# Attention and a feed forward on one Trainium2 core: the last four weight combinations in other places, three sum terms in quads 3 to 5, and raw weights behind q and k in quads 3 and 4

## The chip, the core and the metric

The kernel runs on one core of a Trainium2 chip. TensorE (PE in the profile) multiplies matrices and writes to PSUM. VectorE (DVE), ScalarE (ACT) and GpSimd (POOL) work element by element, and SyncE (SP) issues nearly all transfers between HBM and SBUF. Each engine runs its own instructions in order, and waits for others by semaphores. The metric is device time in microseconds (us); lower is better.

## What is computed

```python
# 8 batches, 12 heads, 448 positions, 64 per head; then 3584 tokens, 768 -> 1024 -> 768
q_n, k_n = rmsnorm(q, g_q), rmsnorm(k, g_k)            # over the 64 of a head
scores = matmul(q_n, k_n^T) / sqrt(64)
attn = softmax(scores);  x = matmul(attn, v)           # heads side by side: 3584 x 768
h = x @ w_in
solu = h * softmax(h)
ln = (solu - mean(solu)) / sqrt(var(solu) + 1e-6) * g_ln
out = ln @ w_out
```

The attention's inputs are float32; w_in and w_out come as float64 and are turned into float32 on the chip.

## The kernel before

**Two stages.** Attention works on 24 *quads* of four heads (m = 0 to 23, three quads per batch). The feed forward then works through 3584 tokens. Both feed forward products are done by a Strassen-like scheme: seven products of half-size blocks in place of eight. For that w_in is kept as seven blocks: three quarters of w_in itself, and four differences of quarters. The differences are made by twelve *combinations* on GpSimd (`combine_in(x)`, x = 0 to 11, L572), subtractions of 128 x 512 elements that have to be done before the first feed forward product.

**A quad** (the loop at L1561). TensorE computes the scores of seven groups of keys (`both_scores`, L870; a group is called 0 to 6), ScalarE takes the exponentials E (L839) straight from PSUM, and TensorE multiplies them by v and accumulates over the seven groups in one PSUM accumulator `o` (`both_values`, L884). There is one buffer for `o`, so the first value product of quad m + 1, which comes behind four scores, has to wait until VectorE has copied `o` of quad m to SBUF as `xo` (`take`, L986). SP then writes it to memory (`store_x`, L993).

**The sums of a row of exponentials** are not divided out here. VectorE adds E tiles of a quad into a few *terms* (`add_pair` L896, `add_to` L902), and TensorE multiplies the terms of one to three quads by ones in one *phase* (`sums`, L941; `end_sums`, L1553) behind the values of the last of them. ScalarE copies the result (`keep_sums`, L957) and SP stores it. In quads 1 to 5 a quad has four terms (E0+E1+E2, E3+E4, E5, E6), from quad 6 on three (E0+E1+E2+E3, E4+E5, E6). Phases stand behind quad 0, quad 2 (quads 1 and 2), quad 4 (3 and 4), quad 5 (5 alone), and then behind every third quad, 8 to 23 (`sums_at`). When a batch is complete its sums are loaded again (`load_sums`), inverted on VectorE (`invert`, L979) and sent to memory (`send_inverses`). x is multiplied by them in the feed forward (`scale`, L1043; x and the inverses of the first tokens are loaded in quads 22 and 23, L1713 to L1720).

**q and k** arrive in eight pieces a quad of 112 KB (`load_piece`, L638). They are squared on ScalarE (`squares`, L687), summed on VectorE (`row_sums`, L692), folded on GpSimd (`fold_sums`, L700), turned into an inverse root on ScalarE and VectorE (`rsqrt_seed` L705, and the norm step `rsqrt_step` L716, four short VectorE instructions), multiplied on GpSimd (`normalise`, L725) and transposed on VectorE (`qk_transpose`, L747). Up to quad 5 the squares and row sums that stand in quad m, between its first scores, are those of quad m + 2. From quad 6 on (`early`) the row sums stand ahead of the scores; the squares for quad m + 3 stand at the end of quad m, from quad 5 on. In quads 3, 4 and 5 ten pieces are loaded each (`load_pieces(10)`, L1646).

**The weights** of w_in come in twelve raw tiles of 512 KB, loaded by `load_next` (L1469) in the quad m for which m + 2 is in `steps_at` (5, 6, 8, 9, ... 21) and converted two quads later by two ScalarE and two VectorE instructions (`convert_w`; the last, `join`, L545 and L546, writes w_in).

**The order is written out by hand.** All of this stands in one program order, and each engine and the SP queue take their part of it in that order. Ahead of a quad's first scores stand, in this order: the load of v for the next quad, the combination if the quad has one (*beside*, L1582 to L1591), `take` of the quad before, its stores, inverses, the raw load (L1603), then the norm step, `normalise` for the next quad, and the q and k pieces. The combinations 0 to 7 stand in quads 11, 12, 14, 15, 17, 18, 20 and 21, one each, *beside* the take: GpSimd first copies one element that VectorE's last work of the quad before has written (`pass_on`, L569), so that the combination begins behind that work, and the program puts `take(m - 1)` ahead of the norm step on VectorE. In the other quads from 6 on the norm step comes ahead of `take`. Quad 22 has four: 8 and 9 without a gate, ahead of the `normalise` of quad 23 (L1639), and 10 and 11 behind the scores' first half (L1678). There the order on VectorE is norm step, then take(21). Quad 23 has none.

Of the kernel before, what the change touches and what calls it, by code (L numbers as in the profile page):

```python
# [366 lines left out]
def fast_path(  # L367
# [32 lines left out]
    NQ = B * NP // 2  # L400
# [171 lines left out]
    def combine_in(x):  # L572
        c, i = divmod(x, 4)
        combine([w_in[k][:, c] for k in range(7)], i)
# [150 lines left out]
    def normalise(n, e=nc.gpsimd):  # L725
        d = st[n]
        y = norms[n // 2]["y"][:, n % 2 * 2 * NB : (n % 2 + 1) * 2 * NB]
        d["qkn"] = work.tile([P, 2 * NB, 32], FP32, tag="qkn", name="qkn", bufs=2)
        e.tensor_tensor(  # L729
            d["qkn"].rearrange("p (s b) d -> p s b d", s=2),  # L730
            d["qk"].rearrange("p s (b d) -> p s b d", d=32),
            y.rearrange("p (s b) -> p s b ()", s=2).to_broadcast([P, 2, NB, 32]),
            OP.mult,
        )
# [718 lines left out]
    EARLY = 6  # L1453
    steps_at = (5, 6, 8, 9, 11, 12, 14, 15, 17, 18, 20, 21)
    combines_at = {11 + 3 * (x // 2) + x % 2: (x,) for x in range(8)}
    combines_first = {22: (8, 9)}
    combines_at[22] = (10, 11)
    sums_at = (2, 4, 5) + tuple(range(8, NQ, 3))
    inverts_at = {4: (0,), 8: (1,), 10: (2,), 14: (3,), 16: (4,), 20: (5,), 22: (6,)}
    wq += [(moe_w_out, c + k, i) for c in range(HF) for k in (0, HF) for i in range(2)]  # L1460
    again = [(w, w.shape[0] // P, i) for w in (moe_w_in, moe_w_out) for i in range(-(-w.shape[0] // P * w.shape[1] // S))]
# [7 lines left out]
    def load_next():  # L1469
        if len(raws) < (n_in if conv is None else len(wq)):  # L1470
            raws.append(load_w(wq[len(raws)]))
# [13 lines left out]
    def load_pieces(n):  # L1485
        nonlocal pieces
        n = min(n, 8 * NQ - pieces)
        for _ in range(n):
            load_piece(pieces)
            pieces += 1  # L1490

    with tc.manual_schedule():
# [68 lines left out]
        for m in range(1, NQ):  # L1561
            a, b = 2 * m, 2 * m + 1
            next1 = m + 1 < NQ
            next2 = m + 2 < NQ
            early = EARLY <= m
            four = m < EARLY

            def score(x):
                unit(lambda: both_scores(m, x))

            def value(x):
                unit(lambda: both_values(m, x))

            if m == 3:
                norm_gain()
            sent = None
            if kept:
                sent = keep_sums(*kept)
                kept = None
            if next1:  # L1580
                load_v(m + 1)
            beside = combines_at.get(m, ()) if m < 22 else ()  # L1582
            if beside:
                if m - 1 in steps_at:
                    step = wq[steps_at.index(m - 1)]
                    pass_on(w_in[(0, 3, 1, 2)[step[1] // HD * 2 + step[2]]][0:1, step[1] % HD, 0:1])
                else:
                    pass_on(quads[m - 1]["terms"][2][1][0:1, 0, 0:1])
                for x in beside:
                    combine_in(x)  # L1590
                take(m - 1)  # L1591
            if early and next1:
                rsqrt_step(norms[m + 1])
            if m > 1 and not beside:
                take(m - 1)
            store_x(m - 1)
            if sent:
                sent()
            for x in inverts_at.get(m - 1, ()):
                send_inverses(x)  # L1600
            for x in inverts_at.get(m, ()):
                load_sums(x)
            if m + 2 in steps_at:  # L1603
                load_next()
            if m == 1:
                score(0)
                score(1)
                score(2)
                rsqrt_seed(norms[2])
                rsqrt_step(norms[2])  # L1610
                normalise(4)
                normalise(5)
                load_pieces(8)
                score(3)
                squares(6)
                row_sums(6)
                qk_transpose(4)
                value(0)
                score(4)
                squares(7)  # L1620
                row_sums(7)
                qk_transpose(5)
                value(1)
                score(5)
                fold_sums(3)
                value(2)
                score(6)
                gains(2)
                rsqrt_seed(norms[3])
                add_pair(m, 0, 1)  # L1630
                add_to(m, 0, 2, nc.vector)
            else:
                if next1:
                    if not early:
                        rsqrt_step(norms[m + 1])
                    if m == 2:
                        add_pair(1, 3, 4)
                        quads[1]["terms"].append((2, quads[1]["E", 5]))
                    for x in combines_first.get(m, ()):  # L1639
                        combine_in(x)  # L1640
                    normalise(a + 2)
                    normalise(b + 2)
                if early:
                    load_pieces(2)
                else:
                    load_pieces(10)  # L1646
                if early and next2:
                    row_sums(a + 4)
                    row_sums(b + 4)
                    load_pieces(6)  # L1650
                if m == NQ - 1:
                    scale(0)
                score(0)
                if m > 2 and not early:
                    squares(a + 4)
                    row_sums(a + 4)
                score(1)
                if next1:
                    qk_transpose(a + 2)
                if m > 2 and not early:  # L1660
                    squares(b + 4)
                    row_sums(b + 4)
                if m == 2:
                    score(2)
                    squares(a + 4)
                    row_sums(a + 4)
                    score(3)
                    squares(b + 4)
                    row_sums(b + 4)
                    qk_transpose(b + 2)  # L1670
                else:
                    if next1:
                        qk_transpose(b + 2)
                    score(2)
                    score(3)
                if next2:
                    fold_sums(m + 2)
                if not beside:  # L1678
                    for x in combines_at.get(m, ()):
                        combine_in(x)  # L1680
                value(0)
                score(4)
                if m in steps_at:
                    low_bits, join, product = convert_w(wq[steps_at.index(m)], raws[steps_at.index(m)])
                    low_bits[0]()
                value(1)
                score(5)
                if m in steps_at:
                    low_bits[1]()
                if next1 and early and m not in sums_at:  # L1690
                    gains(m + 1)
                add_pair(m, 0, 1)
                add_to(m, 0, 2, nc.vector)
                if not four:
                    add_to(m, 0, 3, nc.vector)
                    add_pair(m, 4, 5)
                else:
                    add_pair(m, 3, 4)
                value(2)
                score(6)  # L1700
                if next1 and (not early or m in sums_at):
                    gains(m + 1)
                if m in steps_at:
                    join()
                if next2:
                    rsqrt_seed(norms[m + 2])
                if m + 1 >= EARLY and m + 3 < NQ:
                    squares(a + 6)
                    squares(b + 6)
                if four:  # L1710
                    quads[m]["terms"].append((2, quads[m]["E", 5]))
            quads[m]["terms"].insert(0, (2, quads[m]["E", NK - 1]))
            if m == NQ - 2:  # L1713
                load_x(0)
                load_r(0)
            if m == NQ - 1:
                load_x(1)
                sizes(0)
                block_sums(0, 0)
                block_sums(0, 1)  # L1720
            for x in inverts_at.get(m, ()):
                invert(x)
            for x in range(3, NK):
                value(x)
            waiting.append(m)
            if m in sums_at:
                unit(lambda: None)
                kept = end_sums()
                waiting.clear()
# [62 lines left out]
        for n in range(NS):  # L1792
            base = period * n
            for i, name in enumerate(ORDER):
# [4 lines left out]
                x = HALVES[name][0]  # L1799
# [118 lines left out]
```

## Time and profile before

| | us |
|---|---|
| median of 3 timed runs (lowest, highest) | 786.2 (786.06, 786.36) |
| the profiled execution | 786.86 |
| its span, first to last instruction | 784.2 |
| TensorE busy | 773.3 |
| VectorE busy | 605.9 |
| ScalarE busy | 508.8 |
| GpSimd busy | 485.3 |

The granted TensorE clock is 0.998 over the span, so a TensorE instruction of one shape takes the same time everywhere.

How to read the rows. A row of a timeline has the start in us from the span's start, the duration, the engine, the line of the kernel, the operation, out<-in by the program's names, shapes, and xN where N records are merged. A float32 product leaves two records, so x32 for the scores is 16 products, four groups of keys. A bracket at the end is the idle time of the engine before it and what ended it. A row of groups has the busy time in us, the mean of one in ns, and behind the second bar the idle time before the group with its releasers. In the chain of waits "x64" counts products and weight loads. Names: s are scores, o the accumulator of the values, xo its copy, es the terms of the sums, sm the sums in PSUM, sq squares, ss and part their sums, nx and ny the norm step, qkn and qkT the normalised and the transposed q and k, inv the inverses, raw the float64 weights.

### The profile page before, as it was taken

Reading aid. Unit: us, or ns where it says so; the run is one execution under the profiler, and the core shown is the slowest. Engines: PE = TensorE matmul, PEld = TensorE weight load, DVE = VectorE, ACT = ScalarE, POOL = GpSimd, SP = SyncE. Lnnn points to the kernel's source line nnn. Section 1 sums busy time; section 2 is a strip of 40 time slices with the busy share of each in tenths; the row PEclk is TensorE's granted clock in tenths of the full one; section 3 lists DMA queues with packets and bytes.
Section 4 is the critical chain, followed back from the end, with each engine's and each line's share of the span. In section 5 each row is a group of like instructions: output and inputs, shape, how many; then the busy total and the mean of one; then the engine's idle time right before and its main releaser. Section 6 shows DMA issues by size and latency. Waiting matters only on the chain.

```text
span 784.2 us, 15128 instructions
## 1 busy us (share of the span) xinstructions
PE 773.3 (99%) x5286; PEld 478.8 (61%) x5286; DVE 605.9 (77%) x1061; ACT 508.8 (65%) x833; POOL 485.3 (62%) x633
## 2 busy tenths in 40 slices
PE   8999999999999999999999999999999999999997
PEld 4444444454454444444444444444899999999996
DVE  6876999999999984677788767686697685776944
ACT  6776998988989853787777656556626445464410
POOL 2565343454464542454677688879898777767861
PEclk9999999999999999999999999999999999999999
DMA  9999999999999367577888667773757647456312
GB/s 164 184 182 171 199 181 196 201 201 185 186 194 178 101 152 160 150 180 183 188 182 187 166 146 170 153 184 78 213 162 248 203 148 255 139 191 238 106 61 86
DMA packets 279826, 134.27 MB, mean 171 GB/s; under 512 B 190332, under 2 KB 264892, under 8 KB 279740
## 3 DMA queue, kind: packets, MB, share of 16 engines
q1 hardware_dynamic: 265900, 123.31, 70.4%
q10 hardware_dynamic: 13840, 9.90, 4.4%
q8 instruction: 44, 0.72, 0.4%
q14 instruction: 42, 0.34, 0.2%
HBM read 96.12 MB, written 37.04 MB: 170 GB/s over the span
## 4 chain that ended last, share of the span: by engine, by line
PE 75%; DVE 9%; SPq 6%; POOL 3%; DMA 3%; issue 2%; ACT 1%; DVEq 0%; ACTq 0%; POOLq 0%
PE A L1329 16%; PE A L1103 14%; PE B L1103 9%; PE B L1329 8%; PE o L891 7%; PE s L879 6%; SPq L647 5%; PE D L1103 5%; PE C L1103 5%; PE C L1329 4%; POOL qkn L729 3%; DMA qk<-in_k_dram 2%; DVE es L899 2%; PE sm L951 2%; DVE qkT L750 1%
## 5 line engine op out<-in xcount | busy, mean ns | idle before, releaser
L879 PE MATMUL s<-qkT 64*64 64x448 f32 x1288 | 139.4, 541 | 0.7 <-ACT E L839 0.3
L839 ACT ACTIVATE E<-s 128x896 f32<-128x896 f32 x144 | 124.4, 920 | 22.8 <-PE s L879 22.1
L891 PE MATMUL o<-E,v 64*64 64x448 f32 x1104 | 120.4, 536 | 1.9 <-DVE xo L989 1.9
L729 POOL TENSOR_TENSOR qkn<-qk,ny 128x896 f32<-128x896 f32 x45 | 77.2, 1737 | 71.0 <-DVE ny L723 39.9
L879 PEld LDWEIGHTS s<-qkT 64*64 64x64 f32 x1288 | 65.8, 191 | 60.9 <-issue 39.1
L1329 PE MATMUL A<-w_out,sums 128*128 128x192 f32 x392 | 79.8, 326 | 0.0
L1329 PE MATMUL B<-w_out,sums 128*128 128x192 f32 x392 | 79.8, 326 | 0.0
L891 PEld LDWEIGHTS o<-E,v 64*64 64x64 f32 x1104 | 42.2, 133 | 58.5 <-issue 50.0
L1103 PE MATMUL A<-w_in,xg 128*128 128x512 f32 x168 | 76.8, 593 | 0.0
L1103 PE MATMUL B<-w_in,xsum 128*128 128x512 f32 x168 | 76.7, 592 | 0.0
L1329 PEld LDWEIGHTS B<-w_out,sums 128*128 128x128 f32 x392 | 66.4, 190 | 0.0
L1329 PEld LDWEIGHTS A<-w_out,sums 128*128 128x128 f32 x392 | 66.4, 190 | 0.0
L1103 PEld LDWEIGHTS B<-w_in,xsum 128*128 128x128 f32 x168 | 31.9, 190 | 40.2 <-issue 39.5
L1103 PEld LDWEIGHTS A<-w_in,xg 128*128 128x128 f32 x168 | 31.8, 190 | 40.1 <-issue 38.9
L750 DVE STREAM_TRANSPOSE qkT<-qkn 128x896 f32<-128x896 f32 x46 | 49.9, 1098 | 7.1 <-POOL qkn L729 7.1
L1079 POOL TENSOR_TENSOR xsum<-xg 128x384 f32<-128x384 f32 x14 | 14.7, 1050 | 65.1 <-ACT xsum L1062 42.5
L696 DVE TENSOR_REDUCE part<-sq 128x28 f32<-128x896 f32 x46 | 47.9, 1074 | 9.1 <-ACT sq L690 9.1
L1205 ACT ACTIVATE u<-u,shift,he 128x1024 f32<-128x1024 f32 x28 | 34.8, 1241 | 29.9 <-POOL shift L1201 29.8
L899 DVE TENSOR_TENSOR es<-E 128x896 f32<-128x896 f32 x46 | 50.4, 1097 | 0.1
L905 DVE TENSOR_TENSOR es<-es,E 128x896 f32<-128x896 f32 x41 | 46.9, 1144 | 4.1
L1329 PE MATMUL A<-w_out,s 128*128 128x192 f32 x224 | 45.6, 326 | 0.0
L690 ACT ACTIVATE sq<-qk 128x896 f32<-128x896 f32 x45 | 41.0, 945 | 1.2 <-DMA qk<-in_k_dram 0.5
(173 smaller groups left out, 1660.3 us busy)
## 6 DMA issues: line engine op xcount, KB each, us to landing
ur<-ud SPq DMA_DIRECT2D x60, 256.0 KB, 4.7
ud<-ub SPq DMA_DIRECT2D x112, 128.0 KB, 2.8
xd<-xo SPq DMA_DIRECT2D x48, 224.0 KB, 4.3
qk<-in_q_dram SPq DMA_DIRECT2D x92, 112.0 KB, 4.5
qk<-in_k_dram SPq DMA_DIRECT2D x92, 112.0 KB, 4.0
v<-in_v_dram SPq DMA_DIRECT2D x23, 448.0 KB, 4.2
out_dram<-P SPq DMA_DIRECT2D x19, 384.0 KB, 3.3
raw<-in_moe_w_in_dram SPq DMA_DIRECT2D x12, 512.0 KB, 5.2
```

The costliest lines, as they stand in the source:

```text
L647: nc.sync.dma_start(quads[m]["qk"][g * 32 : g * 32 + 32, s].rearrange("p i (b d) -> p (i b) d", d=32), rows[g // 2, g % 2])
L690: nc.scalar.activation(d["sq"].rearrange("p (s b) d -> p s (b d)", s=2), d["qk"], AF.Square)
L696: nc.vector.tensor_reduce(norms[m]["part"][:, i], st[n]["sq"], AX, OP.add)
L729: e.tensor_tensor(d["qkn"].rearrange("p (s b) d -> p s b d", s=2), d["qk"].rearrange("p s (b d) -> p s b d", d=32), y.rearrange("p (s b) - ...
L750: nc.vector.transpose(d["qkT"].rearrange("p s t -> p (s t)"), d["qkn"].rearrange("p b d -> p (b d)"))
L839: nc.scalar.activation(e, s[:, :, 0:S], AF.Exp)
L879: nc.tensor.matmul(s[i * D : (i + 1) * D, h, 0:S], qkT[hh, i, 1, keys], qkT[hh, i, 0], start=True, stop=True)
L891: nc.tensor.matmul(d["o"][h * D : (h + 1) * D, i, 0:S], d["v"][pp, h, kc], d["E", kc][pp, h], start=kc == 0, stop=kc == NK - 1,)
L899: nc.vector.tensor_tensor(e, d["E", x], d["E", y], OP.add)
L905: engine.tensor_tensor(e, e, d["E", x], OP.add)
L1103: nc.tensor.matmul(k[bank], a[:, c], w_in[i][:, c], start=begin and c == 0, stop=c == HD - 1, skip_group_check=not begin,)
L1329: nc.tensor.matmul(k[bank], a[:, c].rearrange("p a i -> p (a i)"), w_out[:, area, i, c], start=begin and c == 0, stop=c == KC - 1, skip_gr ...
```

## The change

Three edits to the order, all in `fast_path`:

- The combinations 8 to 11: 8 moves to the gated place beside take(21) at the start of quad 22, and with it take(21) goes ahead of the norm step; 9 goes behind quad 22's two `normalise`; 10 and 11 go to the gated place beside take(22) at the start of quad 23.
- Quads 3, 4 and 5 get three terms (one more `add_to` on VectorE, one term less for TensorE), and 4 leaves `sums_at`, so that the three quads are summed in one phase behind quad 5.
- In quads below 6 `load_next` stands behind the ten pieces of q and k. That concerns the first two raw loads, in quads 3 and 4. The pieces, the next v and the stores keep their order among themselves.

```diff
     combines_at = {11 + 3 * (x // 2) + x % 2: (x,) for x in range(8)}
-    combines_first = {22: (8, 9)}
-    combines_at[22] = (10, 11)
-    sums_at = (2, 4, 5) + tuple(range(8, NQ, 3))
+    combines_at[22] = (8,)
+    combines_at[23] = (10, 11)
+    sums_at = (2, 5) + tuple(range(8, NQ, 3))
...
-            four = m < EARLY
+            four = m < 3
...
-            beside = combines_at.get(m, ()) if m < 22 else ()
+            beside = combines_at.get(m, ())
...
-            if m + 2 in steps_at:
+            if early and m + 2 in steps_at:
                 load_next()
...
-                    for x in combines_first.get(m, ()):
-                        combine_in(x)
                     normalise(a + 2)
                     normalise(b + 2)
+                    if m == 22:
+                        combine_in(9)
                 if early:
                     load_pieces(2)
                 else:
                     load_pieces(10)
+                    if m + 2 in steps_at:
+                        load_next()
...
-                if not beside:
-                    for x in combines_at.get(m, ()):
-                        combine_in(x)
                 value(0)
```

## The prediction

> **What bounds the kernel now.** I read the page's groups first, then TensorE's timeline, the chain of waits, and the timelines of VectorE, ScalarE, GpSimd and the DMA queue around the two places where TensorE is late.
>
> ```profile
> L891 PE MATMUL o<-E,v 64*64 64x448 f32 x1104 | 120.4, 536 | 1.9 <-DVE xo L989 1.9
> L729 POOL TENSOR_TENSOR qkn<-qk,ny 128x896 f32<-128x896 f32 x45 | 77.2, 1737 | 71.0 <-DVE ny L723 39.9
> ...
> L1103 PE MATMUL A<-w_in,xg 128*128 128x512 f32 x168 | 76.8, 593 | 0.0
> ```
>
> The number behind the second bar is idle time of the engine before a group. The feed forward's products (L1103) show none, the value products (L891) 1.9 us in all, waiting for xo. So TensorE sets the time, and what is gained before the feed forward stays. Now TensorE's timeline (start, duration; x32 marks the four scores that open a quad, and 302.51 is the first feed forward product):
>
> ```profile
> 50.53 3.30 PE L879 MATMUL s<-qkT 64*64 64x448 f32 x32
> ...
> 61.27 3.19 PE L879 MATMUL s<-qkT 64*64 64x448 f32 x32
> ...
> 75.83 3.30 PE L879 MATMUL s<-qkT 64*64 64x448 f32 x32
> ...
> 88.33 3.30 PE L879 MATMUL s<-qkT 64*64 64x448 f32 x32
> ...
> 98.96 3.19 PE L879 MATMUL s<-qkT 64*64 64x448 f32 x32
> ...
> 123.66 3.30 PE L879 MATMUL s<-qkT 64*64 64x448 f32 x32
> ...
> 159.00 3.30 PE L879 MATMUL s<-qkT 64*64 64x448 f32 x32
> ...
> 264.99 3.30 PE L879 MATMUL s<-qkT 64*64 64x448 f32 x32
> ...
> 275.63 3.19 PE L879 MATMUL s<-qkT 64*64 64x448 f32 x32
> 280.76 0.98 PE L891 MATMUL o<-E,v 64*64 64x448 f32 x8 [1.95 <-DVE xo L989]
> ...
> 288.33 3.19 PE L879 MATMUL s<-qkT 64*64 64x448 f32 x32
> ...
> 302.51 2.84 PE L1103 MATMUL A<-w_in,xg 128*128 128x512 f32 x6
> ```
>
> Quads 9, 10 and 11 with their sums take 159.00 - 123.66 = 35.34 us; I call that the standard group. Quads 3 to 5 take 88.33 - 50.53 = 37.80, which is 2.46 more. Quads 21 to 23 take 302.51 - 264.99 = 37.52, 2.18 more. The change edits exactly these two groups. The most it can give, if both become standard, is 2.46 + 2.18 = 4.64 us.
>
> **Part 1: the sums of quads 3 to 5.** The chain shows the phases of row sums as whole pieces (start, duration):
>
> ```profile
> 72.73 3.17 PE sm L951 x64
> ...
> 86.75 1.65 PE sm L951 x32
> ...
> 120.19 3.54 PE sm L951 x72
> ```
>
> Before, quads 3 and 4 are summed in 3.17 and quad 5 in 1.65, together 4.82. Three quads of three terms (6 to 8) take 3.54. That saves 1.28. A phase also lengthens the scores behind it, 3.30 against 3.19; one phase less saves 0.11.
>
> The price is on VectorE: one more add_to in each of quads 3, 4 and 5.
>
> ```profile
> 61.52 1.09 DVE L989 COPY xo<-o 128x896 f32<-128x896 f32 x1 [0.72 <-PE o L891]
> ...
> 72.00 0.41 DVE L981 RECIPROCAL inv<-inv 128x42 f32<-128x42 f32 x1
> ...
> 78.72 1.09 DVE L696 TENSOR_REDUCE part<-sq 128x28 f32<-128x896 f32 x1 [3.91 <-ACT sq L690]
> ...
> 87.34 0.18 DVE L720 TENSOR_SCALAR nx<-ss 128x56 f32<-128x56 f32 x1
> ...
> 94.42 2.29 DVE L905 TENSOR_TENSOR es<-es,E 128x896 f32<-128x896 f32 x2
> ...
> 99.89 1.08 DVE L989 COPY xo<-o 128x896 f32<-128x896 f32 x1
> ```
>
> Two of them take 2.29, so one is 1.15. In quad 3, VectorE idled 0.72 before take(3), so take(3) ends 0.4 later, at 63.0, and TensorE wants it at 61.27 + 3.0. In quad 4 the additions ended where the reciprocal starts, 72.00; now about 73.15. Adding 0.41 for the reciprocal and 1.08 for take(4) gives 74.6. TensorE would begin quad 5 without a phase and without its stall at 61.27 + 10.53 = 71.8 (10.53 is 98.96 - 88.33 less 0.1) and touches the accumulator after the four scores, 3.0 us later, at 74.8. So this fits by 0.2. In quad 5 the row sums then start behind take(4) and the norm step (four short instructions, 0.9 us), at 75.5 instead of 78.72: the 3.91 of idle time pays 3.2. Of that, 0.7 goes again, because the transposes now wait for GpSimd's normalisation (1.74 by L729, against one row sum of 1.09), and 1.15 goes to quad 5's addition. The norm step of quad 6, at 87.34 before, starts at about 87.3 - 3.2 + 0.7 + 1.15 = 86.0. From there VectorE runs without a gap to take(6), which ended at 100.97 where TensorE wanted it at 98.96 + 3.0 = 101.97: 1.0 us to spare. TensorE moves by 2.46 and VectorE by 1.35, so 1.1 of that 1.0 is used. I take 0.1 us of new stall at the start of quad 7; bounds 0 and 1.2 (if the additions also wait for GpSimd).
>
> **Part 2: the raw weights behind q and k.** What remains of the 2.46 is the stall of quad 4: 75.83 - 61.27 - 3.17 - 10.53 = 0.86.
>
> ```profile
> 51.93 0.46 SPq L513 DMA_DIRECT2D raw<-in_moe_w_in_dram  x1
> ...
> 53.74 6.88 SPq L647 DMA_DIRECT2D qk<-in_k_dram  x4
> ...
> 67.86 4.12 SPq L647 DMA_DIRECT2D qk<-in_k_dram  x4
> ```
>
> ```profile
> 63.72 0.95 ACT L690 ACTIVATE sq<-qk 128x896 f32<-128x896 f32 x1 [0.53 <-DMA qk<-in_k_dram]
> ...
> 77.75 0.94 ACT L690 ACTIVATE sq<-qk 128x896 f32<-128x896 f32 x1
> ```
>
> ```profile
> qk<-in_k_dram SPq DMA_DIRECT2D x92, 112.0 KB, 4.0
> ```
>
> The squares of quad 6 run on ScalarE between the exponentials of quad 4, and wait 0.53 for k pieces. Those four were issued behind a raw load, in 6.88 us, until 60.62; the next four took 4.12. With the raw load behind them they are issued some 3 us sooner, and the squares find them landed. So 0.86 goes: 1.28 + 0.11 + 0.86 = 2.25, and 0.2 that these rows do not name; I keep the group's 2.46.
>
> What is late next is quad 7's k pieces. They stay in quad 4, behind v(5), store_x(3) and the inverses' load, and now in front of the second raw load. Their squares ran at 77.75, 1.92 after quad 5's start, so they are wanted at 71.8 + 1.92 = 73.7. Issued from about 65 (my estimate: two microseconds behind take(3)) in 2.5 to 4.1 us and landing 4.0 later, they are there between 71.5 and 73.2. No stall, with 0.5 us left at the bad end. SP now reaches v(5) early and waits there for TensorE to leave quad 3; the raw transfer fills that wait. The first raw tile is read in quad 5, more than one quad after its new issue, the second in quad 6; nothing waits for them. In quad 4 the second raw load now stands in front of v(6), store_x(4), the inverses and quad 8's last two k pieces, whose squares come only at quad 5's end, beside the sums. I take 0; bounds 0 and 0.86, a stall like the one removed.
>
> **Part 3: the last four combinations.** Rows of quads 21 to 23, VectorE then GpSimd:
>
> ```profile
> 263.37 0.69 DVE L546 SCALAR_TENSOR_TENSOR w_in<-raw,tmp 128x512 uint32<-128x512 uint32 x1
> ...
> 264.30 1.03 DVE L989 COPY xo<-o 128x896 f32<-128x896 f32 x1
> ...
> 266.19 0.22 DVE L723 SCALAR_TENSOR_TENSOR ny<-nx,ny 128x56 f32<-128x56 f32 x1
> ...
> 275.99 0.69 DVE L546 SCALAR_TENSOR_TENSOR w_in<-raw,tmp 128x512 uint32<-128x512 uint32 x1
> ...
> 276.89 1.22 DVE L721 TENSOR_TENSOR nx<-nx,ny 128x56 f32<-128x56 f32 x1
> ...
> 279.49 0.22 DVE L723 SCALAR_TENSOR_TENSOR ny<-nx,ny 128x56 f32<-128x56 f32 x1
> ...
> 285.43 3.18 DVE L905 TENSOR_TENSOR es<-es,E 128x896 f32<-128x896 f32 x2
> ...
> 289.86 1.03 DVE L989 COPY xo<-o 128x896 f32<-128x896 f32 x1
> ```
>
> ```profile
> 264.26 1.27 POOL L567 TENSOR_TENSOR w_in<-w_in,w_in 128x512 f32<-128x512 f32 x1
> ...
> 293.54 1.73 POOL L1079 TENSOR_TENSOR xsum<-xg 128x384 f32<-128x384 f32 x1 [7.07 <-DVE xg L1051]
> ```
>
> In quad 22 combinations 8 and 9 stand first on GpSimd, and VectorE's norm step stands ahead of take(21). A step of 0.22 took 1.22 beside a combination, the next likewise, so take(21) came late and TensorE waited. In quad 21, which has the new order, the copy of take ran beside a combination (264.26) in its usual 1.03. The Trainium skill's page "SBUF — State Buffer", section "Who interferes with whom", says that a VectorE instruction with two SBUF inputs contends with a GpSimd instruction that reads SBUF, and one with at most one SBUF input outside the 2-port modes does not. The 1.22 and the 1.03 agree with it.
>
> So take(21) comes directly behind the join, at 276.7 to 277.7, and TensorE, which wants the accumulator at 275.63 + 3.0, no longer waits: 2.18 goes. What is late next is take(22). In quad 21 the join's end (264.06) to the norm step's end (266.41) was 2.35; from 276.68 that gives 279.0 instead of 279.71, only 0.7 sooner, while TensorE is 2.18 sooner. From the norm step to take(22)'s end it was 290.89 - 279.71 = 11.18, with 0.89 of waiting for combination 11 in it (3.18 against 2.29). Combination 9 alone falls beside the transposes, so I take that off: 279.0 + 11.18 - 0.89 = 289.3. TensorE wants it at 288.33 - 2.18 + 3.0 = 289.15. I take 0.3 of stall; bounds 0 and 1.1 (if combination 9 costs the 0.89 as well).
>
> In quad 23 GpSimd's gate and combinations 10 and 11 take 2 x 1.27 + 0.2 = 2.7 us, where GpSimd idled 7.07 before the block sums; they may delay the scaling of the first x by 1.3, under some 10 us of TensorE's quad 23. Their first reader comes behind 302.51.
>
> **Sum.** 4.64 - 0.1 - 0.3 = 4.24 us. The profiled execution took 786.86 (span 784.2 and 2.66 around it), so it would be 782.6; the three timed runs have a median of 786.2, 0.66 lower, and so I forecast 782.0.
>
> **Rivals.**
> A. Combinations 10 and 11 hold up take(22), which now stands beside them. Then it ends 2.6 us later, the stall moves from quad 22 to quad 23, and Part 3 gives 2.18 - 2.6 - 0.3 = -0.7: 786.2 - 2.36 + 0.7 = 784.5. For it: the order. Against: 1.03 beside 264.26, as a copy out of PSUM. Chance 0.07. By the rule of the Trainium skill quoted above this rival cannot happen; the trace, as far as one overlap shows, agrees.
> B. q and k come late for quad 5 or 6, since TensorE now wants them sooner and the raw loads stand in front of the next quad's transfers. One or two stalls of 0.86: 782.9 to 783.7. For it: 0.5 us of room, and raw loads that slow the issues behind them. Chance 0.14.
> C. Slower: VectorE, gapless from 78.72 to take(6), cannot use its 3.91 of idle time. Then quad 6's norm step comes 3.45 later than before, at 90.8, and take(6) 3.45 - 1.0 = 2.45 behind what TensorE wanted before: instead of gaining 2.46 the group and its neighbour lose 2.45. With 1.88 from Part 3, 786.2 + 2.45 - 1.88 = 786.8; with GpSimd in the way of each addition (1.1 each, 3.3) 790.1. It is slower from the point where that step starts after 90.2. For it: the tight 0.2 in quad 4. Against: the wait was for squares, which come sooner with TensorE. Chance 0.05.
> D. Quads 3 to 5 stay as they are because the stall has another cause and moves on: 786.2 - 1.88 - 1.28 = 783.0. Chance 0.04.
>
> **How the numbers follow.** The forecast has 0.70: 781.4 (nearly all of 4.64, and 0.2 of spread) to 782.9 (0.9 more of the stalls above). B and D reach to 783.7, A to 784.5. The range is 781.2 to 784.2, with half a microsecond for B's bound; it leaves out A and C. About 0.2% (1.6 us) is what a measurement of this kernel can tell from no change. Faster by more: the forecast, B and D, 0.88. Within: A, which stands at the edge, and the lowest part of C, 0.08. Slower: the rest of C, 0.04.
>
> **What would show it.** Right: one sums phase of 3.54 at the end of quad 5, none behind quad 4; 35.3 to 35.6 from quad 3's first score to quad 6's; squares in quad 4 without a wait for k; no TensorE wait for xo in quad 22 and at most 0.5 in quad 23; the first L1103 product near 298.3. Wrong: TensorE waits for xo of over 0.5 in quads 5, 7 or 23, or a squares instruction in quads 4 to 6 that waits for a q or k transfer.

## The result, and the profile after

| | before | changed |
|---|---|---|
| median of 6 runs each, same chip (lowest, highest), us | 786.33 (786.06, 787.01) | 781.87 (781.67, 782.1) |
| the profiled execution, us | 786.86 | 781.84 |
| its span, us | 784.2 | 780.0 |
| TensorE busy, us | 773.3 | 771.0 |

The ratio is 0.9938, with a 95% interval of 0.9927 to 0.9948. In a later set of runs it was 0.9940 (0.9928 to 0.9952). Some executions of the kernel before have a stretch at half clock, which the last section shows; where I compare only executions without it, "at full clock" stands beside the number, and two executions far below full clock (1172.72 us of the kernel before at 0.655, 904.41 us of second_raw_front at 0.85) are in no ratio, median or count.

From the groups of the changed kernel's page: the value products no longer have idle time ahead of them.

```profile
L891 PE MATMUL o<-E,v 64*64 64x448 f32 x1104 | 120.4, 536 | 0.0
```

TensorE's timeline (x32 opens a quad: quads 3 to 7, then 21 to 23, then the first feed forward product):

```profile
50.57 3.30 PE L879 MATMUL s<-qkT 64*64 64x448 f32 x32
...
61.32 3.19 PE L879 MATMUL s<-qkT 64*64 64x448 f32 x32
...
66.58 1.04 PE L879 MATMUL s<-qkT 64*64 64x448 f32 x8
...
71.95 3.19 PE L879 MATMUL s<-qkT 64*64 64x448 f32 x32
...
86.24 3.30 PE L879 MATMUL s<-qkT 64*64 64x448 f32 x32
...
96.87 3.19 PE L879 MATMUL s<-qkT 64*64 64x448 f32 x32
99.88 0.94 PE L891 MATMUL o<-E,v 64*64 64x448 f32 x8
...
262.90 3.30 PE L879 MATMUL s<-qkT 64*64 64x448 f32 x32
...
273.54 3.19 PE L879 MATMUL s<-qkT 64*64 64x448 f32 x32
...
283.50 0.98 PE L891 MATMUL o<-El,v 64*64 64x448 f32 x8
284.30 3.19 PE L879 MATMUL s<-qkT 64*64 64x448 f32 x32
287.32 0.98 PE L891 MATMUL o<-E,v 64*64 64x448 f32 x8
...
298.54 2.84 PE L1103 MATMUL A<-w_in,xg 128*128 128x512 f32 x6
```

Quads 3 to 5 take 86.24 - 50.57 = 35.67 us (37.80 before, so 2.13 less), quads 21 to 23 take 298.54 - 262.90 = 35.64 (37.52, 1.88 less). The feed forward starts at 298.54, 3.97 before its old 302.51, and what follows ends 4.2 earlier. So the two groups carry nearly all of the gain. The chain of waits has one piece of sums behind quad 5, as long as those of every other group of three quads:

```profile
82.76 3.54 PE sm L951 x72
```

VectorE of the changed kernel, first around quads 4 to 7, then around quads 22 and 23:

```profile
73.37 1.03 DVE L989 COPY xo<-o 128x896 f32<-128x896 f32 x1
...
75.23 1.08 DVE L696 TENSOR_REDUCE part<-sq 128x28 f32<-128x896 f32 x1
...
85.85 0.18 DVE L720 TENSOR_SCALAR nx<-ss 128x56 f32<-128x56 f32 x1
...
98.40 1.08 DVE L989 COPY xo<-o 128x896 f32<-128x896 f32 x1
```

```profile
274.56 1.08 DVE L989 COPY xo<-o 128x896 f32<-128x896 f32 x1
275.56 0.60 DVE L720 TENSOR_SCALAR nx<-ss 128x56 f32<-128x56 f32 x1
...
286.24 1.03 DVE L989 COPY xo<-o 128x896 f32<-128x896 f32 x1
```

Take(4) ends at 74.40, before TensorE wants the accumulator at 74.96. The row sums at 75.23 follow without the idle time of 3.91 that stood there before. The copy at 286.24 is take(22). It ran beside combinations 10 and 11 in its usual 1.03 us:

```profile
286.20 3.22 POOL L567 TENSOR_TENSOR w_in<-w_in,w_in 128x512 f32<-128x512 f32 x2
```

ScalarE of the changed kernel, squares in quads 4 and 5 and at quad 5's end, then the end of quad 22:

```profile
63.13 0.94 ACT L690 ACTIVATE sq<-qk 128x896 f32<-128x896 f32 x1
...
73.77 0.94 ACT L690 ACTIVATE sq<-qk 128x896 f32<-128x896 f32 x1
...
83.94 1.79 ACT L690 ACTIVATE sq<-qk 128x896 f32<-128x896 f32 x2 [0.74 <-DMA qk<-in_k_dram]
```

```profile
281.60 1.04 ACT L745 ACTIVATE qkT<-qkT,gcol 128x896 f32<-128x896 f32 x1 [0.88 <-DVE qkT L750]
282.55 0.90 ACT L839 ACTIVATE El<-s 128x896 f32<-128x896 f32 x1
```

No squares between the scores of quads 4 and 5 wait for a transfer any more. Those at quad 5's end do, for 0.74, but they run beside the phase of sums, and TensorE has no idle time there. In quad 22 the gains of quad 23 (L745) stand ahead of the last exponentials El, so the last value product (283.50) is late, and the quad is 10.76 long where a quad without sums is 10.52.

### The profile page after: what moved, and what is told of

The parts are those of the page before. It is cut to its first block, busy times and chain, and to the rows that moved or that the text cites. A ratio compares the mean times of both kernels' runs of the same rounds, so it can differ in the third digit from the quotient of the medians.

```text
span 780.0 us, 15087 instructions
## 1 busy us (share of the span) xinstructions
PE 771.0 (99%) x5262; PEld 478.3 (61%) x5262; DVE 603.6 (77%) x1064; ACT 508.9 (65%) x833; POOL 487.3 (62%) x635
## 4 chain that ended last, share of the span: by engine, by line
PE 94%; SPq 3%; DMA 1%; DVE 0%; POOL 0%; ACT 0%; issue 0%; POOLq 0%; ACTq 0%
PE A L1329 16%; PE o L891 15%; PE s L879 15%; PE A L1103 14%; PE B L1103 9%; PE B L1329 8%; PE D L1103 5%; PE C L1103 5%; PE C L1329 4%; PE sm L951 4%; SPq L647 2%; DMA qk<-in_k_dram 0%; DMA gg<-in_g_q_dram 0%; DVE part L696 0%; POOL ss L706 0%
## 5 line engine op out<-in xcount | busy, mean ns | idle before, releaser
L905 DVE TENSOR_TENSOR es<-es,E 128x896 f32<-128x896 f32 x44 | 49.3, 1120 | 4.4
```

Source lines behind the costliest of these rows:

```text
L905: engine.tensor_tensor(e, e, d["E", x], OP.add)
```

## The experiments

My theory: the gain is three separate ones, a phase of sums (1.48), the stall of quad 4 behind the raw load (up to 0.65) and take(21) (1.9). The rivals: the sums edit alone does it; the raw edit does nothing; in quad 22 it is the order on VectorE alone, or the place of the combinations alone.

All times in us; each ratio is to the kernel before on the same chip. Quad 4 and quad 5 go from first score to first score, and the last digit can differ by one from what the rows give; the last column goes from quad 22's first score to the first feed forward product, in the profiled execution.

| kernel | median (runs) | ratio (95%) | quad 4 | quad 5 | 22 and 23 |
|---|---|---|---|---|---|
| before | 786.33 (6) | | 14.55 | 12.50 | 26.88 |
| changed | 781.87 (6) | 0.9938 (0.9927 to 0.9948) | 10.63 | 14.29 | 25.00 |
| combines_alone | 784.94 (11) | 0.9970 (0.9959 to 0.9981) | 14.23 | 12.50 | 25.08 |
| sums_alone | 785.49 (12) | 0.9986 (0.9973 to 0.9999) | 10.63 | 14.94 | 26.87 |
| raw_alone | 786.27 (11) | 0.9995 (0.9985 to 1.0005) | 13.90 | 12.50 | 26.80 |
| sums_raw | 785.17 (11) | 0.9971 (0.9960 to 0.9982) | 10.63 | 14.28 | 28.54 |
| take_first | 786.67 (12) | 0.9987 (0.9978 to 0.9996) | 13.91 | 12.50 | 26.78 |
| eight_nine_late | 785.99 (12) | 0.9979 (0.9969 to 0.9989) | 14.25 | 12.50 | 26.36 |
| second_raw_front | 782.46 (5) | 0.9937 (0.9922 to 0.9952) | 10.63 | 14.46 | 24.92 |
| gains_late | 781.88 (6) | 0.9929 (0.9916 to 0.9942) | 10.63 | 14.29 | 25.01 |
| after_again | 782.14 (6) | 0.9940 (0.9928 to 0.9952) | 10.63 | 14.28 | 24.91 |
| two_phases | 783.13 (6) | 0.9956 (0.9944 to 0.9968) | 13.15 | 12.13 | 24.97 |
| stall_longer | 789.51 (7) | 1.0031 (1.0020 to 1.0042) | 13.92 | 12.50 | 29.60 |
| four_in_23 | 782.29 (5) | 0.9943 (0.9930 to 0.9955) | 10.63 | 14.28 | 25.10 |

The first four experiments ran on one chip, the next four on another, the last four on the first one again. Single executions of one kernel differ by about 1 us, of which the profiles show the place: quad 1 took 11.05 to 12.36 us, whatever the kernel. The quads' own times are the sharper measure.

**The three edits one by one.** combines_alone is before with all of the edit to the combinations, of which these lines set the places:

```diff
-    combines_first = {22: (8, 9)}
-    combines_at[22] = (10, 11)
+    combines_at[22] = (8,)
+    combines_at[23] = (10, 11)
...
```

> The kernel before with the third edit alone: combination 8 beside take(21), 9 behind quad 22's normalise, 10 and 11 beside take(22); sums and raw loads as before. Theory (three separate costs that add): TensorE's wait of 1.95 for xo in quad 22 goes, 0.3 is left in quads 22 and 23, so 1.9 less than before: 784.4. Rival (the wait moves on to take(22), because without the other edits nothing else is shifted): 786.0 or more, with a wait for xo of over 1 us in quad 23.

The median fell by 1.80 against the executions of before at full clock (786.74, 29 runs), and quads 22 and 23 by 26.88 - 25.08 = 1.80. Part 3 stands by itself.

sums_alone is before with three terms in quads 3 to 5 and one phase:

```diff
-    sums_at = (2, 4, 5) + tuple(range(8, NQ, 3))
+    sums_at = (2, 5) + tuple(range(8, NQ, 3))
...
-            four = m < EARLY
+            four = m < 3
```

> The kernel before with the second edit alone: three terms in quads 3 to 5, one phase; the raw loads stay in front of q and k. Theory of separate costs: 1.28 for 12 fewer products and 0.1 for one phase less, 1.4 in all: 784.9. Rival (loads set the pace of quads 4 to 6): the second raw load still delays quad 7's k pieces, which landed at 75.25 before while TensorE now wants their squares near 74.7; so a stall of 0.5 to 0.9 returns in quad 5 and the gain is 0.5 to 0.9: 785.4 to 785.8.

Quads 4 and 5 took 10.63 + 14.94 = 25.57 in place of 27.05, so 1.48 less, the figure of the separate costs. The median of 785.49 looks like the rival's, but it holds executions with a stretch at half clock; the nine at full clock had 784.96. What the rival said of the wait did come. The stall didn't go: it moved from quad 4 to quad 5, where TensorE and ScalarE (whose squares wait for k) show it:

```profile
76.83 1.04 PE L879 MATMUL s<-qkT 64*64 64x448 f32 x8 [0.33 <-ACT E L839]
```

```profile
75.02 0.95 ACT L690 ACTIVATE sq<-qk 128x896 f32<-128x896 f32 x1 [0.55 <-DMA qk<-in_k_dram]
```

raw_alone is before with only the raw loads moved:

```diff
-            if m + 2 in steps_at:
+            if early and m + 2 in steps_at:
...
+                    if m + 2 in steps_at:
+                        load_next()
```

> The kernel before with the first two raw loads behind the ten pieces of q and k, nothing else. Both theories: the squares of quad 4 no longer wait 0.53 for k, TensorE gains 0.8: 785.5. If the stall had another cause (VectorE or ScalarE late in quad 4): no change, 786.3.

A miss: the time can't be told from that of before (786.27 and 786.74 at full clock, where single executions of either differ by over 1.5). In the profile the edit did what it says, and quad 4 went from 14.55 to 13.90. But that stall isn't the same in each execution. Of the profiles whose code is that of before up to quad 21, quad 4 took 14.55 (before), 14.23 (combines_alone), 14.25 (eight_nine_late), 13.91 (take_first) and 13.92 (stall_longer): 0.65 of stall once, 0.33 and 0.35, and twice next to none, by raw_alone's 13.90.

sums_raw is the changed kernel with the combinations as before.

> The changed kernel without the third edit (combinations as before). Theory of separate costs: quads 3 to 5 gain 2.1, quad 22 keeps its 2.2 of loss: 784.2. If quad 22's wait depends on how late VectorE is after quads 3 to 8: its idle time before the value products in quad 22 differs from 1.95 by over 0.3.

Quads 4 and 5 took 24.91, as in the changed kernel: 1.48 of the sums and 0.65 of the stall. But the median was 1 us above what I expected, and its profile shows why: quad 22 took 14.36 in place of 12.70, because TensorE ran at half clock after its wait for xo. That is the last section's subject. The six executions at full clock had 784.09, as expected.

**What holds take(21) up.** take_first is before with take(21) put ahead of quad 22's norm step, and the combinations where they were:

```diff
+            if m == 22:
+                take(m - 1)
             if early and next1:
                 rsqrt_step(norms[m + 1])
-            if m > 1 and not beside:
+            if m > 1 and not beside and m != 22:
                 take(m - 1)
```

> The kernel before with one thing changed: in quad 22 take(21) stands ahead of the norm step on VectorE; the four combinations stay where they were. Theory (the order on VectorE makes the long wait for xo, and the combinations' lock still delays the norm step): no wait of TensorE for xo in quad 22, but q and k of quad 23 come as late as before, so that about half of the 2.2 us comes back behind the gains or take(22): 0.9 to 1.3 less than before. Rival (the combinations alone are the cause, wherever take stands): no change.

A miss: TensorE didn't wait for take(21) any more, but quads 22 and 23 took 26.78, as before. The wait only moved, to the last value product of quad 22 and to take(22):

```profile
286.89 0.98 PE L891 MATMUL o<-El,v 64*64 64x448 f32 x8 [0.90 <-ACT El L839]
287.69 3.19 PE L879 MATMUL s<-qkT 64*64 64x448 f32 x32
291.59 0.98 PE L891 MATMUL o<-E,v 64*64 64x448 f32 x8 [0.71 <-DVE xo L989]
```

```profile
278.60 1.27 DVE L721 TENSOR_TENSOR nx<-nx,ny 128x56 f32<-128x56 f32 x1
...
286.10 3.16 DVE L905 TENSOR_TENSOR es<-es,E 128x896 f32<-128x896 f32 x2
```

The norm step (1.27 for 0.22) and the additions (3.16 for 2.29) still ran beside combinations and were late. eight_nine_late is before with 8 and 9 behind quad 22's two `normalise`, and the order on VectorE as it was:

```diff
-                    for x in combines_first.get(m, ()):
-                        combine_in(x)
                     normalise(a + 2)
                     normalise(b + 2)
+                    for x in combines_first.get(m, ()):
+                        combine_in(x)
```

> The kernel before with combinations 8 and 9 behind quad 22's two normalise, so that all four stand there; the norm step stays ahead of take(21). Theory: the norm step takes its 0.9 us, take(21) is just in time, and no wait for xo is left in quad 22; but four combinations now stand beside VectorE's additions and hold up take(22) by 1.5 to 2.5 us, of which 0.5 to 1.2 reach TensorE in quad 23: 1.0 to 1.6 less than before. Rival (the order on VectorE is the cause, not the lock): the wait for xo in quad 22 stays over 1 us.

Half a miss: quads 22 and 23 gained 0.52, less than the 1.0 expected. The norm step was short again, and quad 22 took 10.56, but four combinations in a row now lay beside VectorE's additions, and take(22) was late:

```profile
290.65 0.98 PE L891 MATMUL o<-E,v 64*64 64x448 f32 x8 [1.39 <-DVE xo L989]
```

```profile
283.18 4.07 DVE L905 TENSOR_TENSOR es<-es,E 128x896 f32<-128x896 f32 x2
287.16 2.17 DVE L899 TENSOR_TENSOR es<-E 128x896 f32<-128x896 f32 x1
```

So neither half gives the 1.8 while four combinations stay in quad 22. Taking them out of that quad is enough for nearly all of it: four_in_23, below, has none there and keeps the norm step first, and it gains 26.88 - 25.10 = 1.78.

**What is left in the changed kernel.** gains_late puts quad 23's gains behind the last score group of quad 22:

```diff
-                if next1 and early and m not in sums_at:
+                if next1 and early and m not in sums_at and m != 22:
                     gains(m + 1)
...
-                if next1 and (not early or m in sums_at):
+                if next1 and (not early or m in sums_at or m == 22):
                     gains(m + 1)
```

> The changed kernel with one ScalarE instruction moved: in quad 22 the gains of quad 23 stand behind the scores' last group. Theory (two waits end almost together): TensorE no longer waits 0.24 for the last exponentials in quad 22, but take(22), which ended just when TensorE wanted it, is then 0.2 late: same time as the changed kernel within 0.1. Rival (the gains alone hold the rest): 0.24 less than the changed kernel.

Quad 22 took 10.52 (10.76) and quad 23 14.49 (14.24), together 25.01 for 25.00: the wait moved from the gains to take(22). What is left is VectorE's, whichever instruction shows it.

four_in_23 has all four combinations beside take(22):

```diff
-    combines_at[22] = (8,)
-    combines_at[23] = (10, 11)
+    combines_at[23] = (8, 9, 10, 11)
...
-                    if m == 22:
-                        combine_in(9)
```

> The changed kernel, with all of combinations 8 to 11 behind the gate beside take(22) in quad 23 and none in quad 22 (whose norm step is again ahead of take(21)). Theory (what is left of TensorE's waits in quads 22 and 23 comes from combinations 8 and 9 beside VectorE's short instructions, and GpSimd has 7 us free in quad 23): quads 22 and 23 take 24.7 us in place of 25.0, and the time is 0.2 to 0.3 us below after_again. Rival: four combinations in a row, 5.1 us, delay VectorE's additions or the work on the first tokens in quad 23, and it is 0.5 to 1.3 us above after_again.

Neither: quads 22 and 23 took 25.10 for after_again's 24.91, and the medians (782.29 and 782.14) are the same. Four combinations in quad 23 cost TensorE nothing, and that quad was at 14.18 again. So the order on VectorE is not needed for most of the gain. But with no combination beside it, take(21) stands behind the norm step again, and TensorE waits at the start of quad 22, which took 10.92:

```profile
277.19 0.98 PE L891 MATMUL o<-E,v 64*64 64x448 f32 x8 [0.17 <-DVE xo L989]
```

No version beat the changed kernel by more than can be told.

second_raw_front is the changed kernel with the second raw load in front of quad 4's pieces again:

```diff
-            if early and m + 2 in steps_at:
+            if (early or m == 4) and m + 2 in steps_at:
                 load_next()
...
-                    if m + 2 in steps_at:
+                    if m + 2 in steps_at and m != 4:
                         load_next()
```

> The changed kernel with the second raw load (quad 4) back in front of the pieces of q and k; the first stays behind them. Theory (with the sums edit TensorE reaches quad 5 some 3 us earlier, and a raw load in front of quad 7's k pieces is then too early): their squares wait and TensorE loses 0.3 to 0.9 in quad 5, about 0.5 over the changed kernel. Rival (what the run with the sums edit alone lost in quad 5 came from the first raw load): quads 3 to 5 as in the changed kernel, 35.7 from score to score.

Inconclusive in size: quad 5 took 14.46 for 14.29, less than the 0.3 expected. The median was 0.58 above gains_late on the same chip, with five and six runs; 0.70 of the two profiles' difference is quad 1's (11.75 and 11.05).

two_phases is the changed kernel with the sums of quads 3 and 4 finished behind quad 4. after_again is the changed kernel unchanged, for comparison on the same chip.

```diff
-    sums_at = (2, 5) + tuple(range(8, NQ, 3))
+    sums_at = (2, 4, 5) + tuple(range(8, NQ, 3))
```

> The changed kernel once more, on the chip of the three runs below. All theories: about 0.5% less than the kernel before, 781.9 us; quads 22 and 23 together 25.0 us from the first score of quad 22 to the first feed forward product, none of its executions at a mean clock below 0.9965.

> The changed kernel, but the sums of quads 3 and 4 are finished behind quad 4 and those of quad 5 alone behind quad 5 (three terms each, as in the change). The terms are the same number, so that TensorE has the same products in two pieces. My sum: only the restart, 0.1 to 0.2 us more than after_again (782.0). Rival: a phase of its own costs much more than its products, or its copy and store delay the q and k of quad 7, then 0.8 us or more. In the profile: two phases of 2.3 to 2.5 and 1.2 to 1.3 us in place of one of 3.54, and quads 3 to 5 35.8 to 35.9 in place of 35.67.

A miss for my sum: 783.13 - 782.14 = 0.99. The products are the same, in two phases of 2.40 and 1.27 in place of 3.54, but quads 3 to 5 took 10.75 + 13.15 + 12.13 = 36.03, 0.36 more, and quad 7 took 11.09 for 10.52, because TensorE waited for take(6) there:

```profile
100.79 0.98 PE L891 MATMUL o<-E,v 64*64 64x448 f32 x8 [0.34 <-DVE xo L989]
```

```profile
77.41 1.09 DVE L696 TENSOR_REDUCE part<-sq 128x28 f32<-128x896 f32 x1 [2.06 <-ACT sq L690]
...
87.11 0.18 DVE L720 TENSOR_SCALAR nx<-ss 128x56 f32<-128x56 f32 x1
```

The rival's figure came, but by another way than it said: the phase behind quad 4 makes quad 5's squares late, VectorE idles 2.06 us waiting for them, its norm step of quad 6 stands at 87.11 for 85.85, and the short phase behind quad 5 gives it no time to catch up. With one long phase behind quad 5 VectorE works through.

**The half clock.** stall_longer is before with combination 8 issued three times, which makes TensorE's wait in quad 22 longer:

```diff
-                        combine_in(x)
+                        for _ in range(3 if x == 8 else 1):
+                            combine_in(x)
```

> The kernel before, with combination 8 issued three times in a row (the same result each time), so that GpSimd is busy 2.54 us longer at the start of quad 22 and TensorE waits for take(21) longer. Theory of the clock (a wait of TensorE of about two microseconds is at times followed by a stretch at half clock): with a wait of about 3 to 4.5 us the stretch comes in all or nearly all executions, the mean clock is at or below 0.9965 in them, and the time is the longer wait, 1 to 2.5 us, plus about 1.7 us above the undisturbed runs of the kernel before (786.8): 789.5 to 791. Rival (those stretches come from something else than the wait): as many disturbed executions as of the kernel before on the same chip, and 787.8 to 789.3 for the rest.

The wait was 2.98 (before 1.95), a little under the 3 to 4.5 I expected. Six of seven executions had a mean clock of 0.996 or less, with a median of 789.60; the seventh took 788.09. In the profile quad 22 took 15.42, 2.72 more than before: 1.03 of wait, and the rest at half clock. Before had such a clock in 1 of 12 on that chip. So the stretch belongs to the wait; the last section shows it.

## Why the prediction was right, step by step

**Part 1, the sums.** The mechanism held. The saving was forecast at 1.28 + 0.11 and was 1.48: quads 4 and 5 of before without their stall take 27.05 - 0.65 = 26.40, in the changed kernel 24.92. The 0.11 was too small. A phase lengthens the scores behind it by 0.11, but its first product also starts 0.11 later behind the last values than scores do: 82.69 - 81.83 = 0.86 in the changed kernel's quad 5, 71.95 - 71.20 = 0.75 in its quad 4. That makes 1.28 + 0.22 = 1.50. two_phases, with the same products in two pieces, shows 0.36 for a phase's place alone. VectorE's price was paid as forecast: take(4) ended at 74.40 (74.6), the norm step of quad 6 stood at 85.85 (86.0), so the idle time of 3.91 did pay, and rival C fell. The 0.1 of stall in quad 7 didn't come: 96.87 to 99.88 is the usual 3.01. Take(6) ended at 99.48, where I had 99.6, but TensorE was later than I had it, as it moved by 2.13 and not by 2.46.

**The step that was too large** is "I keep the group's 2.46". In it were 0.33 that no edit touched: in each of quads 3, 4 and 5 one score group takes 1.04 in place of 0.93 (the row at 66.58 is one of the three), before and after, and 3 x 0.11 = 0.33. (The granted clock was 1.00 there in both kernels, so products of one shape do not all take the same time at one clock.) Measured was 1.48 + 0.65 = 2.13, and the group's 35.67 lies just above the 35.3 to 35.6 that was to show the forecast right.

**Part 2, the raw weights.** The mechanism held: no squares between the scores of quads 4 and 5 wait for k, and the TensorE stalls of rival B didn't come. By the letter one sign of being wrong did come, the squares at quad 5's end that wait 0.74 for k, but it cost TensorE nothing. One comparison was misread: the four pieces in 4.12, like those in 6.88, stand right behind a raw load, so the two don't show what it costs. First the second raw load of before, then the same two groups of pieces in the changed kernel, with no raw load in front:

```profile
67.38 0.44 SPq L513 DMA_DIRECT2D raw<-in_moe_w_in_dram  x1
```

```profile
53.92 3.06 SPq L647 DMA_DIRECT2D qk<-in_k_dram  x4
...
65.07 3.34 SPq L647 DMA_DIRECT2D qk<-in_k_dram  x4
```

That is 3.06 and 3.34 for 6.88 and 4.12 (raw_alone has 3.33 and 3.38, sums_alone, behind raw loads, 5.49 and 5.62), so the raw load does slow the issues behind it. The 0.86 was too large: 75.83 - 61.27 - 3.17 - 10.53 had 0.21 in it that is not a stall, since quad 4 without one takes 13.90 (raw_alone) and 14.55 - 13.90 = 0.65. And 0.65 is one execution's value; others show 0 to 0.35. A wait seen once in a profile isn't yet a wait of the median. What I had not priced: with the sums changed, the old order of the loads costs 0.65 in quad 5 (sums_alone, one profile), so this edit may be worth more together with Part 1 than by itself; second_raw_front, with only the second load in front, lost 0.17.

**Part 3, the combinations.** 2.18 - 0.3 = 1.88 was forecast, and 1.88 measured. The place was wrong: 0.24 of the rest stands in quad 22 behind the gains and 0.06 in quad 23, where I had it all at take(22). gains_late shows that the two places are worth the same. Rival A fell: take(22) took 1.03 beside two combinations. That also agrees with the rule of the Trainium skill's page "SBUF — State Buffer", section "Who interferes with whom", that the prediction quotes. That neither the order on VectorE nor a later place inside quad 22 is enough by itself I had not worked out; take_first and eight_nine_late show it. The prediction let the wait go because take(21) comes directly behind the join; four_in_23 has 1.78 of the gain with the norm step still first, by the places alone.

**The sum.** The first feed forward product was forecast near 298.3 and came at 298.54. Of the 4.24, 3.97 is there; the median fell by 786.33 - 781.87 = 4.46. The further 0.5 has no row in the two groups and is within what single executions differ by, so the forecast of 782.0 is partly luck: the terms overshot by 0.27. One by one on the same chip the three edits gained 1.80, 1.78 and 0.47 at full clock, 4.05 together, and the changed kernel 786.69 - 782.14 = 4.55, so they add up within that scatter. Rival D (the stall has another cause) fell with raw_alone's profile.

## What to carry to other kernels

Two groups of the same work, of which one takes longer, give the most that an edit can win, but look for what differs between them and is not edited before you take all of it. When a late engine is helped at one wait, follow its next two waits: in four of these experiments the wait, or part of it, only moved. And put a phase that gives another engine time where that engine has work to catch up on.

## What the runs showed of the hardware

**A wait of two microseconds can cost another 1.7 by the clock.** TensorE in sums_raw, then the stretches of its window view, whose third number from the end is the granted clock:

```profile
279.37 1.70 PE L891 MATMUL o<-E,v 64*64 64x448 f32 x8 [1.91 <-DVE xo L989]
280.83 1.74 PE L879 MATMUL s<-qkT 64*64 64x448 f32 x8
282.32 1.23 PE L891 MATMUL o<-E,v 64*64 64x448 f32 x8
```

```profile
278.00:280.00 2.00, 0.63 (x4) 0.24 (x8) 1.28 (x3) 0.62 (x1) 1.61 (x1) 0.87 0.00 0
280.00:282.00 2.00, 2.00 (x16) 0.80 (x12) 1.34 (x2) 0.00 (x0) 2.00 (x3) 0.50 0.65 140
282.00:284.00 2.00, 2.00 (x20) 0.84 (x16) 1.92 (x2) 0.92 (x1) 1.92 (x2) 0.77 0.82 204
```

The same in stall_longer, TensorE and then the window view:

```profile
282.03 1.01 PE L891 MATMUL o<-E,v 64*64 64x448 f32 x8 [2.98 <-DVE xo L989]
282.83 1.70 PE L879 MATMUL s<-qkT 64*64 64x448 f32 x8
```

```profile
282.00:284.00 2.00, 1.97 (x16) 0.92 (x20) 0.07 (x1) 0.00 (x0) 2.00 (x3) 0.71 0.33 72
284.00:286.00 2.00, 2.00 (x16) 0.75 (x12) 1.46 (x2) 0.92 (x1) 2.00 (x2) 0.50 0.87 192
286.00:288.00 2.00, 2.00 (x27) 0.87 (x24) 1.90 (x3) 0.97 (x2) 1.92 (x2) 0.93 0.97 310
```

Products that take 0.93 take 1.70 to 1.74. In sums_raw (0.13 + 0.50 + 0.23) x 2 = 1.72 us are lost, in stall_longer (0.29 + 0.50 + 0.07) x 2 = 1.72 as well: both are 3.44 us at half clock. It doesn't follow each time: the profile of before has its wait of 1.95, which ends at 280.76, and a clock of 1.00 behind it. Counting executions with a mean clock of 0.996 or less (1.72 of 784 is 0.0022, and the others have 0.997 to 1.000), I find 18 of 69 of before (6 of 35, 11 of 22 and 1 of 12 in three sets), 3 of 12 of sums_alone, 5 of 11 of sums_raw, and 6 of 7 with the wait of 2.98. raw_alone keeps before's wait too and had none in 11. The kernels without that wait had it in none of 69. The limit is narrow, since the last microseconds of each kernel are at half clock too (from 780.91 on in the profile of before, which is all that its mean of 0.998 holds). Two more executions of before and two of sums_alone, at 0.997, were also 1.1 to 3.8 us above their kernel's median at full clock, so the counts may be low. So the changed kernel also loses this risk, and its gain should be larger where before has the stretch more often. The Trainium skill's page "TensorE: Matmul & The Clock Gate", Part 1, section "What's actually happening", tells of a gate that falls to half after an idle window of about 3.4 us and opens again after a busy one of that length, and the window is free-running. The length of 3.44 agrees with one such window. On the idle time the measurement differs and decides: here the clock fell after 1.91 us of waiting, so less than a whole window was enough.

The traces show where the wait has to lie. In all fourteen profiles the time from the first full clock to each drop is a whole number of stretches of 3.413 us: 80 of them in sums_raw, 81 in stall_longer, and 226 to 228 where the clock drops only at the kernel's end. So the clock is set window by window on a fixed grid. Two of these windows and the ones behind them, in sums_raw and then in raw_alone (the second number is TensorE's busy time):

```profile
276.08:279.49 3.41, 1.50 (x20) 0.54 (x16) 3.16 (x4) 2.54 (x4) 2.93 (x3) 1.00 0.34 126
279.50:282.90 3.40, 3.40 (x20) 1.18 (x23) 2.24 (x3) 0.28 (x1) 3.40 (x3) 0.50 0.61 143
```

```profile
277.47:280.88 3.41, 1.54 (x20) 0.58 (x16) 2.62 (x4) 2.03 (x3) 2.93 (x3) 1.00 0.20 74
280.88:284.30 3.42, 3.42 (x40) 1.65 (x36) 2.79 (x3) 1.70 (x2) 3.34 (x4) 1.00 0.75 156
```

TensorE was idle for 3.41 - 1.50 = 1.91 of the one window and for 1.87 of the other, and only the first was followed by half clock. In before and sums_alone an edge of the grid splits the wait, so that no window has more than 1.61 and 1.33 of it. In all fourteen profiles, once the clock has first been full, every window with 1.91 or more of idle time is followed by a drop, and none with 1.87 or less. So a wait of 1.9 brings the stretch only where no edge splits it, which fits that it came in some executions, and one slightly shorter need not bring it at all, which fits raw_alone's none in 11.

**GpSimd beside VectorE slows both.** Combination 8 beside VectorE's copy out of PSUM took 1.27 in the changed kernel. Two beside VectorE's scaling took 3.22, and four beside its additions 7.54 in eight_nine_late, where two additions took 4.07 for 2.29. The TENSOR_SCALAR at 275.56, with one SBUF input, took 0.60 for 0.18 while combination 8 ran, and ended at 276.16 when the combination had ended at 276.11; copies out of PSUM took 1.03 to 1.08 beside them.
